# Gate and up projections ahead of the query projection in a decode kernel

## The chip, the cores and the metric

The kernel runs on one core of one Trainium2 chip. The metric is the device time of one execution in microseconds (us); three runs of the kernel before gave 228.95, 229.00 and 229.19, median 229.0. A profile is of one execution. MB are millions of bytes.

## What is computed

Two parallel branches of one decode step share a layer norm: attention over the last 4096 cached positions, with 32 query heads on 8 key/value heads, and a gated MLP. All data are float32, batch B = 2, one token, D = 512, head size 128, F = 1792.

```python
xn = _layernorm(x, axis=-1)
# attention
q = (xn @ wq).reshape(B, Sq, 32, 128)
k = k_cache[:, :, Sk - 4096:, :]        # each kv head serves 4 query heads
v = v_cache[:, :, Sk - 4096:, :]
p = softmax(einsum(q, k) * 128 ** -0.5)
attn = (p @ v).reshape(B, Sq, 4096) @ wo
# gated MLP
gate, up = xn @ W_gate, xn @ W_up
h = gate * (gate > 0) * up
return x + attn + h @ W_down
```

## The kernel before

**The stream.** Nearly all bytes are weights and cache tiles that are read once: wq in two halves of 4096 KB, w_gate and w_up of 3584 KB each, eight k tiles and eight v tiles of 4096 KB, w_down, and wo. They all go through one pool of four buffers, `ring` (L53, RING = 4), in program order, and SP issues their DMAs in that order (`load`, L69 to 72). The fifth load takes the first buffer, and so on in turn: a load waits on SP until the work that reads the buffer's old tile is done, and all later loads wait behind it. Only x comes on ACT's queue (L106).

**The opening.** DVE, ACT and PE do the layer norm; eight small matmuls (L193) transpose xn into xnT in two layouts. Then PE multiplies xnT with wq, 16 matmuls per half (L205), into two PSUM tiles. In the profile each float32 matmul shows as two records, so a half is "x32". For each tile r, ACT or DVE copies it to SBUF (qs, L213), four PE transposes turn it (qt, L216), and 16 small copies, in turn on ACT and DVE, place it into qz (L227), the zero-padded weights of the score matmuls. Then come gate and up: 16 matmuls each (L235), a copy on ACT (L240), and on DVE the gating (L242, L244) and a transpose into hT (L245). hT is not read until the projection with w_down near the end (L431).

**The attention loop.** There are four groups g (kv heads 0 to 3 or 4 to 7, of one batch row), each with two k tiles and two v tiles. `keys(g, a, ...)` transposes a k tile on DVE in two pieces (kT, L259), and after each piece PE does eight score matmuls with qz (L264; "x16" in the profile). When both k tiles of a group are through, `softmax(g)` goes from DVE over PE and ACT (L276 to 296) and `turn(g)` turns the probabilities on DVE (L302, L308). `values(g, a, v)` does the matmuls with a v tile one group later (L327). Each engine works in program order. Group 0's two k tiles come first, then for g = 1, 2, 3 and a = 0, 1 a k tile of group g and a v tile of group g - 1, then the last two v tiles, w_down and wo.

**Which slot is whose.** In the kernel before, wq's two halves, w_gate and w_up are loads 1 to 4; k0 a=0, k0 a=1, k1 a=0 and v0 a=0 are loads 5 to 8 and take their buffers. Load 9 (k1 a=1) takes the buffer of k0 a=0 when DVE has transposed it, load 10 (v0 a=1) that of k0 a=1, load 11 (k2 a=0) that of k1 a=0, load 12 (v1 a=0) that of v0 a=0 when PE has used it. Names such as k2_0 below mean group 2, a = 0.

**The end.** The projections with w_down and wo accumulate in PSUM (L431, L435); wo's last rows come in small pieces (L450, L456); DVE copies the result (L469) and SP writes it out (L471).

Of the kernel before, what the change touches and what calls it, by code (L numbers as in the profile page):

```python
# [9 lines left out]
F32 = mybir.dt.float32  # L10
AF = mybir.ActivationFunctionType
ALU = mybir.AluOpType
# [8 lines left out]
def kernel(  # L21
# [12 lines left out]
    nc = tc.nc  # L34
    P = 128
# [6 lines left out]
    KC = D // P  # L42
# [3 lines left out]
    Q = 4  # L46
# [8 lines left out]
    FB = F // P  # L55
    FQ = F // Q
# [5 lines left out]
    work = ctx.enter_context(tc.tile_pool(name="work", bufs=2))  # L62
    ps_kt = ctx.enter_context(tc.tile_pool(name="ps_kt", bufs=3, space=PSUM))
# [5 lines left out]
    def load(name, src, shape):  # L69
        t = ring.tile(shape, F32, name=name, tag="ring")  # L70
        nc.sync.dma_start(t, src)
        return t


    def load_wq(m):
        src = wq[m * 2 * P:(m + 1) * 2 * P, :].rearrange("(p k) f -> p k f", p=P)
        return load(f"wq{m}", src, [P, 2, HQ * DH])

    def load_ff(w, name):
        return load(name, w.rearrange("(p k) f -> p k f", p=P), [P, KC, F])  # L80
# [23 lines left out]
    x2 = const.tile([B, D], F32, name="x2")  # L104
    for half in (slice(0, D // 2), slice(D // 2, D)):
        nc.scalar.dma_start(x2[:, half], x[:, 0, half])  # L106
    wqt = [load_wq(m) for m in range(2)]

    ident = const.tile([P, P], F32, name="ident")
# [13 lines left out]
    hT = const.tile([P, FB, 32], F32, name="hT")  # L123
# [34 lines left out]
    for h in range(2):  # L158
        nc.vector.tensor_reduce(
            out=by_h[:, :, h], in_=ident[:, PK * h:PK * h + PK].rearrange("p (x t k) -> p t k x", t=NP, k=REP),  # L160
            op=ALU.add, axis=AX.X,
# [25 lines left out]
    for kc in range(KC):  # L187
        m, k = divmod(kc, 2)
# [7 lines left out]
    xnT = const.tile([P, 2, KC, 32], F32, name="xnT")  # L196
    nc.vector.tensor_copy(xnT, xt_ps)


    q_ps = [ps_kt.tile([P, 512], F32, name=f"q_ps{r}", tag="kt") for r in range(R)]  # L200
    for kc in range(KC):
        for r in range(R):
            for c in range(C):
# [2 lines left out]
                    q_ps[r][32 * c:32 * c + 32, :], xnT[:, 0, kc, :], wqt[kc // 2][:, kc % 2, n * 512:(n + 1) * 512],  # L206
                    start=(kc == 0), stop=(kc == KC - 1),
                )
    gw = load_ff(w_gate, "wg")
    uw = load_ff(w_up, "wu")  # L210
    for r in range(R):
        qs = work.tile([P, 512], F32, name=f"qs{r}", tag="qs")
        (nc.vector.tensor_copy if r else nc.scalar.copy)(qs, q_ps[r])  # L213
# [5 lines left out]
        for m in range(NB):  # L219
            src = qt[32 * m:32 * m + 32, :, :, 0].rearrange("p i (t h) b -> p b t h i", h=2)  # L220
            for x in range(Q):
                d = qz[32 * x:32 * x + 32, r * B:r * B + B, m]
                dst = bass.AP(
                    tensor=d.tensor, offset=d.offset + x * TK,
                    ap=[d.ap[0], d.ap[1], [64 + REP, NP], [32, 2], [1, REP]],
                )
                (nc.vector.tensor_copy if x % 2 else nc.scalar.copy)(dst, src)  # L227


    g_ps = ps_kt.tile([P, FQ], F32, name="g_ps", tag="kt")  # L230
    u_ps = ps_kt.tile([P, FQ], F32, name="u_ps", tag="kt")
    for dst, wt in ((g_ps, gw), (u_ps, uw)):
        for kc in range(KC):
            for c in range(Q):
                nc.tensor.matmul(  # L235
                    dst[32 * c:32 * c + 32, :], xnT[:, 1, kc, :], wt[:, kc, c * FQ:(c + 1) * FQ],
                    start=(kc == 0), stop=(kc == KC - 1),
                )
    gs = work.tile([P, FQ], F32, name="gs", tag="qs")
    nc.scalar.copy(gs, g_ps)  # L240
    gr = gs
    nc.vector.scalar_tensor_tensor(gr, gs, 0.0, gs, op0=ALU.is_gt, op1=ALU.mult)  # L242
    hh = work.tile([P, FQ], F32, name="hh", tag="qs")
    nc.vector.tensor_tensor(hh, gr, u_ps, op=ALU.mult)  # L244
    nc.vector.transpose(hT, hh.rearrange("p (w k) -> p k w", k=FB))  # L245

    ss, pts = {}, {}
# [197 lines left out]
    for r, cuts in ((0, (0, NJ)), (1, (0, 4, 8, 12, 14, 15))):  # L447
        wt = ring.tile([P, NJ, D], F32, name=f"wo{r}", tag="ring")
# [53 lines left out]
```

## Time and profile before

| what | value |
|---|---|
| median of three runs | 229.0 us |
| the profiled execution's own time | 228.95 us |
| its span in the trace | 227.2 us |
| PE busy | 129.8 us (57%) |
| DVE busy | 118.7 us (52%) |
| ACT busy | 14.3 us (6%) |
| bytes read from HBM | 94.90 MB |

Times in the trace count from the start of the span. PE, DVE, ACT and POOL are the engines for matmuls, vector work, activations and the rest; PEld is PE's loading of weights; "SPq" rows are DMAs that SP issues, with the time at which it does. In a timeline row stand the start, the length, the engine, the line, out<-in, the shapes and the count; in square brackets the engine's idle time before it and what ended it. In a row of windows stand the bounds, the length, the busy time of PE, PEld, DVE, ACT and POOL with the number of their instructions, then PE's granted clock (1.00 is full), the DMA engines' mean share (packets are counted where they begin, so a short window can go over 1) and the GB/s.

### The profile page before, as it was taken

What the parts mean: (1) busy time and instruction counts of PE and PEld (TensorE: products, weight loads), DVE (VectorE), ACT (ScalarE), POOL (GpSimd) and SP (SyncE); (2) the same over time, 40 slices, a digit from 0 to 9 for tenths busy, and PEclk for the clock granted to TensorE, in tenths of its full rate; (3) what the DMA queues carried; (4) which work ended last, traced back from release to release, by engine and by line L of the source; (5) the groups of instructions that cost most, each with busy time, mean ns of one, the idle gap of its engine ahead of it and who ended that gap; (6) DMA issues with size and microseconds to landing.
All of it is one profiled execution on the core that took longest, in us unless ns stands there. A gap on an engine that the chain in (4) does not pass through costs nothing.

```text
span 227.2 us, 2137 instructions
## 1 busy us (share of the span) xinstructions
PE 129.8 (57%) x896; PEld 39.2 (17%) x896; DVE 118.7 (52%) x160; ACT 14.3 (6%) x41; POOL 4.2 (2%) x14
## 2 busy tenths in 40 slices
PE   0195754803656003886815984607937644988694
PEld 0161220200101001221201321101501201221313
DVE  2400142039892399973599894699269286013000
ACT  2000231000000500000200000200000110000001
POOL 7000000000000000000000000000000000000000
PEclk9999979675876655896675899955996996599769
DMA  7999999999999999999999999999999999999992
GB/s 277 462 398 421 454 434 413 462 421 415 456 440 398 450 462 404 424 462 404 424 462 415 421 456 433 407 450 450 415 427 456 410 424 462 408 428 453 385 415 74
DMA packets 4212, 95.03 MB, mean 418 GB/s; under 512 B 488, under 2 KB 748, under 8 KB 1004
## 3 DMA queue, kind: packets, MB, share of 16 engines
q1 hardware_dynamic: 4196, 94.90, 97.3%
q8 instruction: 7, 0.11, 0.2%
q14 instruction: 1, 0.01, 0.0%
q10 hardware_dynamic: 8, 0.00, 0.0%
HBM read 94.90 MB, written 0.00 MB: 418 GB/s over the span
## 4 chain that ended last, share of the span: by engine, by line
DMA 50%; DVE 26%; PE 17%; issue 3%; ACT 2%; SPq 0%; DVEq 0%; ACTq 0%
DMA k<-in_A_k_cache_dram 28%; DVE kT L259 17%; DMA wo<-in_A_wo_dram 13%; DMA wq<-in_A_wq_dram 9%; PE s L264 7%; DVE pt L308 4%; PE yw_ps L431 3%; PE o L327 3%; PE q_ps L205 2%; ACT pz L296 1%; DVE pT L302 1%; PE y_ps L435 1%; DVE m L276 1%; DVE on L336 1%; PE oa L347 1%
## 5 line engine op out<-in xcount | busy, mean ns | idle before, releaser
L264 PE MATMUL s<-kT,qz 128*32 128x512 f32 x256 | 44.5, 822 | 55.8 <-DVE kT L259 55.7
L259 DVE STREAM_TRANSPOSE kT<-k 128x4096 f32<-128x4096 f32 x16 | 70.5, 4428 | 10.7 <-DMA k<-in_A_k_cache_dram 10.6
L327 PE MATMUL o<-v,pt 128*32 128x512 f32 x256 | 34.5, 672 | 0.0
L264 PEld LDWEIGHTS s<-kT,qz 128*32 128x32 f32 x256 | 8.8, 130 | 84.9 <-issue 60.1
L308 DVE COPY pt<-pT 32x256 f32<-32x256 f32 x64 | 18.2, 284 | 1.0
L347 PE MATMUL oa<-on,pick 128*16 128x512 f32 x16 | 10.1, 721 | 6.9 <-DVE on L336 6.9
L327 PEld LDWEIGHTS o<-v,pt 128*32 128x32 f32 x256 | 9.6, 121 | 19.4 <-issue 19.4
L336 DVE TENSOR_TENSOR on<-o,own_u 128x512 f32<-128x512 f32 x8 | 5.4, 676 | 12.7 <-PE o L327 12.6
L227 DVE COPY qz<-qt 32x32 f32<-32x32 f32 x16 | 3.0, 187 | 16.7 <-ACT qz L227 16.7
L296 ACT ACTIVATE pz<-s,nm 64x512 f32<-64x512 f32 x8 | 5.9, 732 | 80.0 <-DVE nm L290 79.8
L205 PE MATMUL q_ps<-wq,xnT 128*32 128x512 f32 x64 | 8.8, 698 | 3.0 <-DMA wq<-in_A_wq_dram 2.5
L193 PE MATMUL xt_ps<-rep,xc 2*128 2x32 f32 x16 | 3.7, 402 | 10.7 <-DVE rep L186 10.7
L302 DVE STREAM_TRANSPOSE pT<-pz 128x1024 f32<-128x1024 f32 x4 | 5.0, 1245 | 8.3 <-ACT pz L296 8.3
L431 PE MATMUL yw_ps<-wo,oT 128*2 128x512 f32 x48 | 7.9, 831 | 1.9 <-DMA wo<-in_A_wo_dram 1.9
L276 DVE TENSOR_REDUCE m<-s 128x1 f32<-128x512 f32 x4 | 2.8, 692 | 11.6 <-PE s L264 11.6
L469 DVE COPY yo<-y_ps 128x128 f32<-128x128 f32 x1 | 0.3, 290 | 16.4 <-PE y_ps L435 16.4
L235 PE MATMUL u_ps<-wu,xnT 128*32 128x448 f32 x32 | 4.9, 781 | 4.3 <-DMA wu<-in_B_W_up_dram 4.3
L193 PEld LDWEIGHTS xt_ps<-rep,xc 2*128 2x128 f32 x16 | 3.6, 319 | 10.7 <-DVE rep L186 10.7
L235 PE MATMUL g_ps<-wg,xnT 128*32 128x448 f32 x32 | 4.9, 769 | 0.0
L244 DVE TENSOR_TENSOR hh<-gs,u_ps 128x448 f32<-128x448 f32 x1 | 0.6, 620 | 7.9 <-PE u_ps L235 7.9
L347 PEld LDWEIGHTS oa<-on,pick 128*16 128x16 f32 x16 | 1.6, 112 | 15.2 <-DVE on L336 9.8
L365 PEld LDWEIGHTS op<-osb,spread 16*128 16x128 f32 x32 | 3.7, 186 | 1.8 <-issue 1.8
(72 smaller groups left out, 56.4 us busy)
## 6 DMA issues: line engine op xcount, KB each, us to landing
k<-in_A_k_cache_dram SPq DMA_DIRECT2D x8, 4096.0 KB, 24.4
v<-in_A_v_cache_dram SPq DMA_DIRECT2D x8, 4096.0 KB, 28.9
wq<-in_A_wq_dram SPq DMA_DIRECT2D x2, 4096.0 KB, 16.7
wo<-in_A_wo_dram SPq DMA_DIRECT2D x1, 4096.0 KB
wg<-in_B_W_gate_dram SPq DMA_DIRECT2D x1, 3584.0 KB, 29.3
wu<-in_B_W_up_dram SPq DMA_DIRECT2D x1, 3584.0 KB, 38.6
wd<-in_B_W_down_dram SPq DMA_DIRECT2D x1, 3584.0 KB, 28.0
wo<-in_A_wo_dram SPq DMA_DIRECT2D x3, 1024.0 KB, 18.8
```

Source lines behind the costliest of these rows:

```text
L193: nc.tensor.matmul(xt_ps[:, v, kc, :], lhsT, rep16.rearrange("r s b -> r (s b)"), start=True, stop=True)
L205: nc.tensor.matmul(q_ps[r][32 * c:32 * c + 32, :], xnT[:, 0, kc, :], wqt[kc // 2][:, kc % 2, n * 512:(n + 1) * 512], start=(kc == 0), stop ...
L235: nc.tensor.matmul(dst[32 * c:32 * c + 32, :], xnT[:, 1, kc, :], wt[:, kc, c * FQ:(c + 1) * FQ], start=(kc == 0), stop=(kc == KC - 1),)
L259: nc.vector.transpose(kt.rearrange("p j m i -> p j (m i)"), src)
L264: nc.tensor.matmul(ss[g][32 * q:32 * q + 32, :], qz[:, g, 2 * mh + m, a, h], kt[:, JS * s1:JS * s1 + JS, m, h::2], start=(a == 0 and mh == ...
L296: nc.scalar.activation(pv[o, :, :, h], ss[g][o].rearrange("p (j i) -> p j i", j=JS), AF.Exp, bias=nm[o], scale=SCALE, accum_out=l[o],)
L302: nc.vector.transpose(pT.rearrange("p j x t k -> p (j x t k)"), pz.rearrange("p j s -> p (j s)"))
L308: nc.vector.tensor_copy(pts[g][32 * x:32 * x + 32, :, s1, :, h], pT[q:q + 32, :, x].rearrange("p j t k -> p t j k"))
L327: nc.tensor.matmul(o[32 * q:32 * q + 32, :], pts[g][:, a, s1, j:j + 4].rearrange("p u h k -> p (u h k)"), v[:, lo:lo + 512], start=(s1 == ...
L336: nc.vector.tensor_tensor(ons[a], o.rearrange("p (u d) -> p u d", u=4), own_u[:, :, None].to_broadcast([P, 4, P]), op=ALU.mult)
L347: nc.tensor.matmul(oa[g].rearrange("h u d -> h (u d)"), pick[:, 8 - 8 * a:24 - 8 * a], ons[a].rearrange("p u d -> p (u d)"), start=(a == 0 ...
L431: nc.tensor.matmul(yw_ps[32 * c:32 * c + B, :], lhsT, w, start=(n < Q), stop=(n >= wide - Q))
```

## The change

The loads of w_gate and w_up go ahead of those of wq, and the matmuls and the elementwise steps of gate and up go ahead of the query projection. Nothing is added or left out; the lines of the steps move, by one or two elsewhere.

```diff
     for half in (slice(0, D // 2), slice(D // 2, D)):
         nc.scalar.dma_start(x2[:, half], x[:, 0, half])
+    gw = load_ff(w_gate, "wg")
+    uw = load_ff(w_up, "wu")
     wqt = [load_wq(m) for m in range(2)]
...
     nc.vector.tensor_copy(xnT, xt_ps)
+    g_ps = ps_kt.tile([P, FQ], F32, name="g_ps", tag="kt")
+    u_ps = ps_kt.tile([P, FQ], F32, name="u_ps", tag="kt")
+    for dst, wt in ((g_ps, gw), (u_ps, uw)):
+        for kc in range(KC):
+            for c in range(Q):
+                nc.tensor.matmul(
+                    dst[32 * c:32 * c + 32, :], xnT[:, 1, kc, :], wt[:, kc, c * FQ:(c + 1) * FQ],
+                    start=(kc == 0), stop=(kc == KC - 1),
+                )
+    gs = work.tile([P, FQ], F32, name="gs", tag="qs")
+    nc.scalar.copy(gs, g_ps)
+    gr = gs
+    nc.vector.scalar_tensor_tensor(gr, gs, 0.0, gs, op0=ALU.is_gt, op1=ALU.mult)
+    hh = work.tile([P, FQ], F32, name="hh", tag="qs")
+    nc.vector.tensor_tensor(hh, gr, u_ps, op=ALU.mult)
+    nc.vector.transpose(hT, hh.rearrange("p (w k) -> p k w", k=FB))
     q_ps = [ps_kt.tile([P, 512], F32, name=f"q_ps{r}", tag="kt") for r in range(R)]
...
-    gw = load_ff(w_gate, "wg")
-    uw = load_ff(w_up, "wu")
     for r in range(R):
         qs = work.tile([P, 512], F32, name=f"qs{r}", tag="qs")
...
-    g_ps = ps_kt.tile([P, FQ], F32, name="g_ps", tag="kt")
...
-    nc.vector.transpose(hT, hh.rearrange("p (w k) -> p k w", k=FB))
```

The start of SP's queue, as a difference; wq_81 to wq_87 are the two halves of wq, wg and wu the gate and up weights, and k_0_272 and k_1_295 the two k tiles of group 0:

```order
-L71 DMA wq_81<-in_A_wq_dram 128x8192
-L71 DMA wq_83<-in_A_wq_dram 128x8192
 L71 DMA wg<-in_B_W_gate_dram 128x7168
 L71 DMA wu<-in_B_W_up_dram 128x7168
+L71 DMA wq_85<-in_A_wq_dram 128x8192
+L71 DMA wq_87<-in_A_wq_dram 128x8192
 L71 DMA k_0_272<-in_A_k_cache_dram 128x1x8192
 L71 DMA k_1_295<-in_A_k_cache_dram 128x1x8192
```

The halves of wq have moved from the first two places to the third and fourth, so the ring's first two buffers now hold w_gate and w_up; all later loads stand as before.

DVE from the copy of xnT to the first two k transposes, before; qt and q_ps are the PSUM tiles of the query, kT_0_0 and kT_0_1 the pieces of group 0's first k tile:

```order
L197 COPY xnT<-xt_ps 128x256
L227 COPY qz<-qt_188 32x2x2x2x4 x8
L213 COPY qs_209<-q_ps_149 128x512
L227 COPY qz<-qt_211 32x2x2x2x4 x8
L242 SCALAR_TENSOR_TENSOR gs<-gs 128x448
L244 TENSOR_TENSOR hh<-gs,u_ps 128x448
L245 STREAM_TRANSPOSE hT<-hh 128x448
L259 STREAM_TRANSPOSE kT_0_0_275<-k_0_272 128x4096
L259 STREAM_TRANSPOSE kT_0_1_285<-k_0_272 128x4096
```

And the same place on DVE in the changed kernel:

```order
L199 COPY xnT<-xt_ps 128x256
L214 SCALAR_TENSOR_TENSOR gs<-gs 128x448
L216 TENSOR_TENSOR hh<-gs,u_ps 128x448
L217 STREAM_TRANSPOSE hT<-hh 128x448
L245 COPY qz<-qt_228 32x2x2x2x4 x8
L231 COPY qs_249<-q_ps_193 128x512
L245 COPY qz<-qt_251 32x2x2x2x4 x8
L258 STREAM_TRANSPOSE kT_0_0_275<-k_0_272 128x4096
L258 STREAM_TRANSPOSE kT_0_1_285<-k_0_272 128x4096
```

The 16 qz copies and the qs copy now stand between hT and the k transposes, where they had stood ahead of the three steps of gate and up.

More of the change, by code (lines that the diff above doesn't have):

```diff
@@ L227 @@
                 (nc.vector.tensor_copy if x % 2 else nc.scalar.copy)(dst, src)
-    g_ps = ps_kt.tile([P, FQ], F32, name="g_ps", tag="kt")
[L231 to L244, printed above, removed]
-    nc.vector.transpose(hT, hh.rearrange("p (w k) -> p k w", k=FB))
     ss, pts = {}, {}
```

## The prediction

> **What bounds the kernel now.** I read the page first: utilisation in 40 slices, DMA queues, chain.
>
> ```profile
> span 227.2 us, 2137 instructions
> DMA  7999999999999999999999999999999999999992
> GB/s 277 462 398 421 454 434 413 462 421 415 456 440 398 450 462 404 424 462 404 424 462 415 421 456 433 407 450 450 415 427 456 410 424 462 408 428 453 385 415 74
> q1 hardware_dynamic: 4196, 94.90, 97.3%
> DMA 50%; DVE 26%; PE 17%; issue 3%; ACT 2%; SPq 0%; DVEq 0%; ACTq 0%
> ```
>
> The DMA digits are 9 from the second slice to the last but one. The chain names DVE for 26%, but that only says who released a ring slot; the transfer it released queued behind others. Next, windows: long ones for the rate, and ones that begin at zero to count what had been moved when a load was first used.
>
> ```profile
> 0.00:22.55 22.55, 8.85 (x48) 4.72 (x48) 4.16 (x17) 1.58 (x2) 4.20 (x14) 1.00 0.94 393
> 0.00:60.20 60.20, 27.85 (x176) 10.00 (x180) 18.80 (x39) 5.53 (x20) 4.20 (x14) 0.86 0.98 418
> 0.00:92.91 92.91, 39.83 (x235) 12.17 (x235) 43.52 (x65) 8.38 (x25) 4.20 (x14) 0.78 0.99 423
> 22.00:92.00 70.00, 30.64 (x187) 7.45 (x187) 38.45 (x47) 6.80 (x23) 0.00 (x0) 0.72 1.00 432
> 92.00:202.00 110.00, 70.80 (x471) 20.09 (x468) 74.14 (x92) 5.05 (x13) 0.00 (x0) 0.81 1.00 433
> ```
>
> The last column is GB/s: 432 and 433 over two long stretches, DMA share 1.00. The rate does not depend on what PE or DVE do. The end hangs on the same stream: the last weight load for y_ps waits 0.16 us for a piece of wo, and the output leaves right behind it.
>
> ```profile
> 223.90 0.13 PEld L435 LDWEIGHTS y_ps<-wo,oT_rows 128*17 128x17 f32 x8 [0.16 <-DMA wo<-in_A_wo_dram]
> 224.60 0.69 SPq L471 DMA_DIRECT2D out_dram<-yo  x1
> ```
>
> So the time is the start of the stream, 94.90 MB at its rate, and a fixed tail. The change moves no byte count. It can matter only if the queue runs dry, and for that I read the SP timeline (issue times) and the sizes.
>
> ```profile
> wq<-in_A_wq_dram SPq DMA_DIRECT2D x2, 4096.0 KB, 16.7
> wg<-in_B_W_gate_dram SPq DMA_DIRECT2D x1, 3584.0 KB, 29.3
> 0.73 0.85 SPq L71 DMA_DIRECT2D wq<-in_A_wq_dram  x2
> 20.11 17.04 SPq L71 DMA_DIRECT2D k<-in_A_k_cache_dram  x3
> 45.80 0.54 SPq L71 DMA_DIRECT2D v<-in_A_v_cache_dram  x1
> 59.27 0.53 SPq L71 DMA_DIRECT2D k<-in_A_k_cache_dram  x1
> 69.03 0.53 SPq L71 DMA_DIRECT2D v<-in_A_v_cache_dram  x1
> 92.91 0.53 SPq L71 DMA_DIRECT2D k<-in_A_k_cache_dram  x1
> 98.56 0.54 SPq L71 DMA_DIRECT2D v<-in_A_v_cache_dram  x1
> ```
>
> In MB of a million bytes, wq halves, k and v tiles are 4.19 each, w_gate and w_up 3.67 each. Before the issue at 92.91 (k2_0, first half of group 2) the queue had been given 15.73 for the four weights and 6 x 4.19 for k and v, 40.89 in all. By 92.91 it had begun 423 x 92.91 = 39.30. What remains, 1.59 MB, lasts 3.7 us at 432. Done the same way, the next issue (98.56) has 45.09 MB queued against about 41.7 begun, 7.8 us; at 59.27 it is 32.50 against 418 x 59.27 = 24.8, 18 us. **The issue of k2_0 is the one thin place, with 3.7 us.** It waits for a slot that DVE frees.
>
> **The change, part by part.**
>
> *The four weight loads in another order.* Same four transfers, same sum of 15.73 MB, all issued without a wait near 0.7 to 2.7 us. Whatever lands fourth lands when w_up did. Cost: 0 to the stream.
>
> *The gate/up matmuls first.* They take over the time that the first q half had, under the loading of wq. Their ACT and DVE steps are then done while DVE would stand still; nobody waits for hT before the end of the kernel. The three slots freed by PE in this stage come within a few us of their old times, against 18 us and more of queued bytes: cost 0.
>
> *The q chain last.* Here lies the cost. These are the rows, PE and DVE timeline:
>
> ```profile
> 22.55 3.64 PE L205 MATMUL q_ps<-wq,xnT 128*32 128x512 f32 x32 [2.51 <-DMA wq<-in_A_wq_dram]
> 35.02 0.20 DVE L227 COPY qz<-qt 32x32 f32<-32x32 f32 x1 [0.24 <-ACT qz L227]
> 40.83 4.91 PE L235 MATMUL u_ps<-wu,xnT 128*32 128x448 f32 x32 [4.28 <-DMA wu<-in_B_W_up_dram]
> 50.47 8.77 DVE L259 STREAM_TRANSPOSE kT<-k 128x4096 f32<-128x4096 f32 x2 [3.07 <-DMA k<-in_A_k_cache_dram]
> 60.23 8.77 DVE L259 STREAM_TRANSPOSE kT<-k 128x4096 f32<-128x4096 f32 x2 [0.99 <-DMA k<-in_A_k_cache_dram]
> 59.39 2.05 PE L264 MATMUL s<-kT,qz 128*32 128x512 f32 x16 [0.69 <-DVE kT L259]
> 69.06 3.64 PE L264 MATMUL s<-kT,qz 128*32 128x512 f32 x16 [1.49 <-DVE kT L259]
> 84.11 13.10 DVE L259 STREAM_TRANSPOSE kT<-k 128x4096 f32<-128x4096 f32 x3
> 40.00:42.00 2.00, 1.17 (x12) 0.42 (x16) 0.00 (x0) 0.00 (x0) 0.00 (x0) 0.97 1.10 475
> 42.00:44.00 2.00, 2.00 (x16) 0.65 (x12) 0.00 (x0) 0.00 (x0) 0.00 (x0) 0.50 1.18 508
> 70.00:72.00 2.00, 2.00 (x16) 0.30 (x8) 0.00 (x0) 0.00 (x0) 0.00 (x0) 0.50 1.21 524
> ```
>
> 1. wq's second half now lands at 40.8, where w_up did. Its 32 records are 512 wide. The nearest row is u_ps: 4.91 x 512/448 = 5.6 us, so q ends at 46.4. The bounds are the full-clock row, 3.64 us (44.5), and twice that (48.1): the granted clock (third column from the end) is 0.97 and then 0.50 inside the u_ps burst.
> 2. From the end of q to the last qz copy it took 35.22 - 26.19 = 9.0 us, a ping-pong of ACT and DVE with two rounds of transposes. It was hidden under weight loading. Now it ends at 55.4, and DVE, which runs in order, cannot begin the k transposes at 50.47 as before. Queued behind it on DVE are all kT transposes, and PE and SP wait for those.
> 3. The first two transposes (8.77) end at 64.2 instead of 59.24; the second tile, there since 60.2, follows at once and ends at 73.0 instead of 69.0. One gap of 0.99 us has swallowed part. DVE is now 4.0 us late.
> 4. The last score batch before the softmax took 3.64 us at clock 0.50; at full clock such a batch takes 2.05. Shifted by 4 us against the clock, it may be either: lateness 4.0 or 2.4. I take the middle, 3.2, as the batches in the trace come in both lengths.
> 5. The softmax chain and the next two transposes are unchanged, so k2_0 goes out at 92.91 + 3.2 = 96.1.
>
> The Trainium skill, "TensorE: Matmul & The Clock Gate" (Part 1), says that the gate judges activity in free-running windows of about 3.4 us and that an idle one halves the clock. By that rule q's second half, after more than 4 us of idleness, would run one window at half speed and the rest at full, 3.4 + 1.9 = 5.3 us instead of my 5.6; the row above, with its drop at 42 and not at 40.83, agrees with free-running windows.
>
> **Is 96.1 late?** When an empty queue is given work, packets do not start at once: issue at 0.73, first packets at 1.75 to 2.25 (rows of a quarter microsecond; the last one is of the second packets).
>
> ```profile
> 1.75:2.00 0.25, 0.00 (x0) 0.00 (x0) 0.00 (x0) 0.25 (x1) 0.25 (x1) 1.00 4.39 1180
> 2.00:2.25 0.25, 0.00 (x0) 0.00 (x0) 0.00 (x0) 0.25 (x1) 0.25 (x1) 1.00 1.89 524
> 3.75:4.00 0.25, 0.00 (x0) 0.00 (x0) 0.00 (x0) 0.00 (x0) 0.25 (x2) 1.00 2.73 1180
> ```
>
> That is 1.2 us. An average DMA engine runs out at 92.91 + 3.7 = 96.6, so an issue by 95.4 costs it nothing: margin 2.5 us. The Trainium skill, "DMA: Bandwidth & Descriptors" (Latency and other measured facts), gives about 0.6 us to the first byte; by it the margin would be 3.1. No run here shows 0.6.
>
> But the engines are not in step. At 22.55, when both wq halves (8.39 MB) had landed, 8.86 had been begun, 0.47 more. At 60.20, when six loads (24.12 MB) had landed, it was 25.16, 1.04 more. One partition's row of a tile is 4096/128 = 32 KB; one such packet on each of 16 engines is 0.52 MB, 1.2 us at 432. So from then on the slowest engine is about one packet behind the mean. Its own row would be dry only 1.2 us later: margin 3.7. A load is complete when its slowest engine is, and so is the kernel. With 3.2 us of lateness the faster engines pause for 0.7 us, the slowest does not pause, and the end stays.
>
> *Afterwards.* DVE stays about 3 us late up to the long wait below, 6.58 us for a k tile, which takes it all; from there the stream sets the pace again.
>
> ```profile
> 166.84 4.45 DVE L259 STREAM_TRANSPOSE kT<-k 128x4096 f32<-128x4096 f32 x1 [6.58 <-DMA k<-in_A_k_cache_dram]
> ```
>
> **Sum:** stream 0 + weights 0 + q chain 0 (3.2 of lateness against 3.7 of margin), so the profiled 228.95 us (span 227.2 and 1.75 around it) stays. It is the lowest of three runs; the median is 229.0, and that is the forecast. Its own range is 228.6 to 229.4, which is the 0.2% that a measurement of this kernel can tell from no change.
>
> **The rivals.**
>
> *A bubble in the stream at 97 us (slower).* If the mean engine counts, because lagging engines catch up while others pause or because the lag lies elsewhere, every us of lateness over 2.5 is lost to the end: nothing later makes up for lost DMA time at share 1.00. Lateness 3.2 gives 0.7, so 229.7. Lateness 4.0 gives 1.5, and the refill may add 0.7, since the second packets at the start came 1.9 us behind the first (3.75 to 4.00) instead of 1.2: 230.5 to 231.2. It decides from a lateness of about 3.0 on. For it: the only thin place of the trace. Against it: the lag counted above, and a last score batch that may get shorter.
>
> *q wholly at half clock (slower still).* 7.3 us for q's second half make the lateness up to 5.7; even the slowest engine loses 2.0: 231. Against it: the full-clock stretch at the head of the u_ps burst.
>
> *An earlier start (faster).* The x rows share the queues with the first weight, whose rows shrink from 32 KB to 3584/128 = 28, so x and xnT may come some tenths earlier, and the first slots come free earlier. At share 1.00 that has no taker; at the most a tighter start gives 0.6 us: 228.4.
>
> **How the numbers follow.** No change that can be told: 0.55. Bubble: 0.33. Half clock: 0.05. Faster: 0.07. So faster 0.07, same 0.55, slower 0.38. The range goes from 228.5 to 230.8; it leaves out the half-clock case, the worst fifth of the bubble case and half of the faster one, about 0.15.
>
> **What would show it.** In the profile after: last qz copy near 55.4 and the first kT right behind it; second kT pair ending near 73; the k issue that stood at 92.91 near 96; windows near 97 that keep their GB/s, or show a hole in the bubble case; DVE's wait for k of 6.58 shrunk by the lateness; last piece of wo at the same 223.9. I am wrong if k2_0 goes out before 94 or after 97.5, if a hole shows and the end moves by as much, or if the end moves without one.

## The result: slower by 0.75%

The changed kernel took 230.68 us (median of six runs, 230.28 to 231.73), the kernel before 229.03 (six runs, 228.92 to 229.19). The ratio is 1.0075, with a 95% interval from 1.006 to 1.009. The forecast had been no change, 229.0; the time lies in the stated range and in the rival's, a bubble in the stream at 97 us (229.7 to 231.2).

### The profile after

First the page of the changed kernel. The profiled execution took 231.73 us, the slowest of the six, so it shows the loss at its largest.

```profile
span 229.8 us, 2136 instructions
DMA  7999999999999999899999999999999999999990
GB/s 260 449 414 434 450 442 439 399 451 445 439 399 446 445 439 405 368 411 399 456 445 428 402 456 439 433 402 456 439 416 422 456 436 397 448 444 431 384 385 27
q1 hardware_dynamic: 4196, 94.90, 96.6%
```

There is one 8 among the nines, in slice 17, from 91.9 to 97.7 us; its 368 GB/s is the lowest figure between the first slice and the last; the ends of the kernel apart, no other is below 397. Next SP's issues in the same trace, around the one that matters.

```profile
47.24 0.54 SPq L71 DMA_DIRECT2D v<-in_A_v_cache_dram  x1
65.49 0.54 SPq L71 DMA_DIRECT2D k<-in_A_k_cache_dram  x1
74.14 0.54 SPq L71 DMA_DIRECT2D v<-in_A_v_cache_dram  x1
96.42 0.54 SPq L71 DMA_DIRECT2D k<-in_A_k_cache_dram  x1
102.46 0.54 SPq L71 DMA_DIRECT2D v<-in_A_v_cache_dram  x1
```

k2_0 goes out at 96.42 instead of 92.91, 3.5 us late. What the stream did there is read from windows. The first two rows are of the kernel before, up to 90 us and from 90 to 110 us:

```profile
0.00:90.00 90.00, 37.49 (x227) 11.95 (x231) 40.61 (x64) 8.38 (x25) 4.20 (x14) 0.79 0.99 424
90.00:110.00 20.00, 15.32 (x105) 4.36 (x101) 13.59 (x8) 0.46 (x1) 0.00 (x0) 0.84 0.98 422
```

And the same two stretches of the changed kernel:

```profile
0.00:90.00 90.00, 37.80 (x219) 12.21 (x219) 36.98 (x63) 8.37 (x25) 4.21 (x14) 0.76 0.99 424
90.00:110.00 20.00, 14.76 (x94) 3.66 (x98) 15.76 (x5) 0.00 (x0) 0.00 (x0) 0.76 0.96 399
```

Up to 90 us both kernels have moved the same, at 424 GB/s. Then the changed one moves 23 GB/s less over 20 us, 0.46 MB or 1.1 us of stream. That is the hole. Now the steps that lead to it, on PE and DVE of the changed kernel.

```profile
30.17 6.54 PE L225 MATMUL q_ps<-wq,xnT 128*32 128x512 f32 x32 [6.50 <-DMA wq<-in_A_wq_dram]
40.85 6.32 PE L225 MATMUL q_ps<-wq,xnT 128*32 128x512 f32 x32 [4.14 <-DMA wq<-in_A_wq_dram]
74.17 2.06 PE L263 MATMUL s<-kT,qz 128*32 128x512 f32 x16 [2.27 <-DVE kT L258]
56.47 0.20 DVE L245 COPY qz<-qt 32x32 f32<-32x32 f32 x1 [0.24 <-ACT qz L245]
56.69 17.42 DVE L258 STREAM_TRANSPOSE kT<-k 128x4096 f32<-128x4096 f32 x4
87.62 13.10 DVE L258 STREAM_TRANSPOSE kT<-k 128x4096 f32<-128x4096 f32 x3
169.43 4.45 DVE L258 STREAM_TRANSPOSE kT<-k 128x4096 f32<-128x4096 f32 x1 [2.73 <-DMA k<-in_A_k_cache_dram]
```

The last qz copy ends at 56.67, the first k transpose follows at once, and all four of group 0 run without a gap, to 74.11. The last score batch is a short one, 2.06 us. The transposes that free k2_0's slot begin at 87.62, where they had begun at 84.11. Much later DVE waits 2.73 us for a k tile, where it had waited 6.58. Last, the end of the trace.

```profile
226.59 0.13 PEld L434 LDWEIGHTS y_ps<-wo,oT_rows 128*17 128x17 f32 x8 [0.18 <-DMA wo<-in_A_wo_dram]
227.28 0.68 SPq L470 DMA_DIRECT2D out_dram<-yo  x1
```

The last piece of wo is waited for until 226.59 instead of 223.90: 2.7 us, as much as this execution is longer (2.78). So the end still hangs on the stream, and lost more than the hole of 1.1.

### The profile page after: what moved, and what is told of

It is laid out like the page before. It is cut to its first block, busy times and chain, and to the rows that moved or that the text cites. A ratio compares the mean times of both kernels' runs of the same rounds, so it can differ in the third digit from the quotient of the medians.

```text
span 229.8 us, 2136 instructions
## 1 busy us (share of the span) xinstructions
PE 132.2 (58%) x896; PEld 39.0 (17%) x896; DVE 118.8 (52%) x160; ACT 14.3 (6%) x41; POOL 4.2 (2%) x14
## 4 chain that ended last, share of the span: by engine, by line
DMA 38%; DVE 31%; PE 19%; issue 4%; ACT 4%; SPq 1%; DVEq 0%; ACTq 0%
DVE kT L258 19%; DMA wq<-in_A_wq_dram 17%; DMA k<-in_A_k_cache_dram 12%; DMA wo<-in_A_wo_dram 10%; PE s L263 7%; DVE pt L307 6%; PE o L326 5%; PE q_ps L225 3%; ACT pz L295 2%; DVE pT L301 2%; PE oa L346 2%; DVE qz L245 1%; ACT qz L245 1%; DVE on L335 1%; DVE m L275 1%
## 5 line engine op out<-in xcount | busy, mean ns | idle before, releaser
L326 PE MATMUL o<-v,pt 128*32 128x512 f32 x256 | 33.0, 648 | 0.0
L225 PE MATMUL q_ps<-wq,xnT 128*32 128x512 f32 x64 | 12.9, 978 | 10.6 <-DMA wq<-in_A_wq_dram 10.6
L346 PE MATMUL oa<-on,pick 128*16 128x512 f32 x16 | 10.8, 766 | 6.9 <-DVE on L335 6.9
L326 PEld LDWEIGHTS o<-v,pt 128*32 128x32 f32 x256 | 8.8, 117 | 18.9 <-issue 18.8
L430 PE MATMUL yw_ps<-wo,oT 128*2 128x512 f32 x48 | 7.0, 748 | 2.1 <-DMA wo<-in_A_wo_dram 2.1
L225 PEld LDWEIGHTS q_ps<-wq,xnT 128*32 128x32 f32 x64 | 2.8, 168 | 20.5 <-DMA wq<-in_A_wq_dram 12.7
L207 PE MATMUL g_ps<-wg,xnT 128*32 128x448 f32 x32 | 5.4, 850 | 0.5 <-DVE xnT L199 0.5
L234 PE MATMUL qt<-ident,qs 128*128 128x128 f32 x8 | 1.7, 356 | 4.4 <-DVE qs L231 4.4
L364 PE MATMUL op<-osb,spread 16*128 16x32 f32 x32 | 3.9, 273 | 0.0
## 6 DMA issues: line engine op xcount, KB each, us to landing
wg<-in_B_W_gate_dram SPq DMA_DIRECT2D x1, 3584.0 KB, 11.2
```

The costliest lines, as they stand in the source:

```text
L225: nc.tensor.matmul(q_ps[r][32 * c:32 * c + 32, :], xnT[:, 0, kc, :], wqt[kc // 2][:, kc % 2, n * 512:(n + 1) * 512], start=(kc == 0), stop ...
L326: nc.tensor.matmul(o[32 * q:32 * q + 32, :], pts[g][:, a, s1, j:j + 4].rearrange("p u h k -> p (u h k)"), v[:, lo:lo + 512], start=(s1 == ...
L346: nc.tensor.matmul(oa[g].rearrange("h u d -> h (u d)"), pick[:, 8 - 8 * a:24 - 8 * a], ons[a].rearrange("p u d -> p (u d)"), start=(a == 0 ...
L364: nc.tensor.matmul(op, spread.rearrange("h k e -> h (k e)")[:, NE - 1 - e:NE - 1 - e + P], osb[r][:, :, e * NJ:(e + 1) * NJ].rearrange("h ...
```

## The experiments

**Theory A** says that the stream runs dry near 97 us because k2_0 is issued late, and that each engine's own pause counts. A second form of it, with which I had forecast, has the margin of the slowest engine, 3.7 us. **Theory B** says that the new order of loads or matmuls costs something as such. All comparisons are with runs of the kernel before on the same chip.

### The lateness taken out of the changed kernel: q1act

The second tile's part of the query chain goes to ACT alone; all else is the changed kernel.

```diff
-        (nc.vector.tensor_copy if r else nc.scalar.copy)(qs, q_ps[r])
+        nc.scalar.copy(qs, q_ps[r])
...
-                (nc.vector.tensor_copy if x % 2 else nc.scalar.copy)(dst, src)
+                (nc.vector.tensor_copy if x % 2 and r == 0 else nc.scalar.copy)(dst, src)
```

> The changed kernel, with the second half of the query chain (the qs1 copy and its 16 small qz copies) given to ACT alone, so that DVE is free for the first k transpose after the first eight qz copies, near 51.3 us instead of 56.7. The lateness of the k2_0 issue (96.42 in the changed kernel, 92.91 before) should fall from 3.5 to about 0 to 1 us. Theory A (the stream runs dry at 97 us because k2_0 is issued late): no hole at 97, 229.0 to 229.4 us, ratio to the kernel before within 0.998 to 1.002. Theory B (the cost comes from the new order of the loads or of the matmuls as such, and k2_0 only happens to be late): 230.3 to 230.9 us, as the changed kernel.

It took 229.03 us against 229.13, ratio 0.9998 (0.999 to 1.0007). The rows are DVE's first k transposes, SP's issue of k2_0 and the window at the hole:

```profile
51.25 8.77 DVE L258 STREAM_TRANSPOSE kT<-k 128x4096 f32<-128x4096 f32 x2
92.50 0.54 SPq L71 DMA_DIRECT2D k<-in_A_k_cache_dram  x1
90.00:110.00 20.00, 15.43 (x105) 3.91 (x101) 13.19 (x8) 0.41 (x1) 0.00 (x0) 0.82 0.99 426
```

DVE is free 5.4 us earlier, k2_0 is on time, the hole is gone, and with it the whole loss, though w_gate and w_up are still loaded and used first. Theory B falls for the change as made.

The control, the same edit in the kernel before (before_q1act):

> Control for q1act: the kernel before with the same edit (second half of the query chain on ACT alone). There the chain is hidden under the loading of the weights, so k2_0 stays near 92.9. Theory A: 229.0 to 229.2 us, ratio 0.998 to 1.002. If the edit itself saved time, this would come out at 228.5 or less, and the cure in q1act would not speak for the late issue alone.

229.03 against 228.99, ratio 1.0002 (0.9993 to 1.0011). The edit gains nothing of its own.

### The lateness put into the kernel before: the late series

Before the transposes that free k2_0's slot, DVE repeats the hT transpose n times, 0.97 us each; loads and opening stay as before.

```diff
     softmax(0)
     turn(0)
+    for _ in range(n):
+        nc.vector.transpose(hT, hh.rearrange("p (w k) -> p k w", k=FB))
```

> The kernel before with one idle 0.94 us repeat of the hT transpose ahead of the k transposes that free the slot of k2_0; issue near 93.9 at the latest. Theory A (the stream runs dry, every engine for itself; late2 lost in some executions and not in others): inside the margin, 229.0 to 229.2 us and a narrow spread. Theory A with a margin of 3.7: the same.

> The kernel before, with two idle repeats of the 0.94 us hT transpose on DVE between the first softmax and the k transposes that free the slot of k2_0: k2_0 goes out about 1.9 us later, near 94.9. Both theories: under the margin of the mean engine (2.5 us), so 229.0 us, ratio 0.998 to 1.002. A loss here would say that the margin was reckoned too wide.

> Three repeats, 2.9 us. Between late2 (229.25) and late4 (230.93). Theory A with every engine's own pause counting: 229.8 to 230.6 us. With the slowest engine's margin of 3.7 us: 229.0 to 229.2.

> As late2 with four repeats: k2_0 about 3.9 us late, near 96.8, a little later than in the changed kernel, with the loads and the opening as before. Theory A, margin 2.5 us for every engine and a refill of up to 0.7: 230.4 to 231.1 us, with a hole of about 1.4 us in the stream at 97. Theory A with a margin of 3.7, the slowest engine's: 229.2 us. Theory B: 229.0 to 229.2 us.

> As late2 with six repeats: k2_0 about 5.8 us late, near 98.7. Theory A, margin 2.5 for every engine: 3.3 us of hole and up to 0.7 of refill, 232.3 to 233.0 us. With the slowest engine's margin of 3.7: 231.1 us. Theory B: the kernel before has no other cost here, 229.0 to 229.3 us.

> Ten repeats, 9.7 us, or 8.1 where the last score batch comes out short as it did in late4 and late6. late6 went out at 97.0, 4.1 us late, and lost 2.2 us, so lateness less 2.0 goes to the end. Theory A: 6.1 to 7.7 us lost, 235.1 to 236.8 us, a hole of 6 us or more, and a tail after the hole no longer than the kernel before has, since all engines start again together. With the slowest engine's margin of 3.7: 233.4 to 235.1.

The issue time, the GB/s from 90 to 110 us and the one time are of the profiled execution.

| n | k2_0 issued (late by) | GB/s 90 to 110 | that execution, us | median, us | before, us | ratio (95%) |
|---|---|---|---|---|---|---|
| 1 | 93.62 (0.7) | 422 | 229.19 | 229.04 | 229.03 | 1.0005 (0.9996 to 1.0014) |
| 2 | 94.51 (1.6) | 415 | 231.11 | 229.25 | 229.13 | 1.0029 (1.0006 to 1.0051) |
| 3 | 94.15 (1.2) | 419 | 230.29 | 230.18 | 229.03 | 1.0054 (1.0035 to 1.0073) |
| 4 | 94.93 (2.0) | 419 | 231.18 | 230.93 | 229.13 | 1.0074 (1.0054 to 1.0094) |
| 6 | 97.01 (4.1) | 386 | 231.02 | 231.36 | 229.13 | 1.0103 (1.0081 to 1.0125) |
| 10 | 102.43 (9.5) | 271 | 236.32 | 234.98 | 229.03 | 1.0273 (1.0253 to 1.0294) |

The issue rows and windows of two of them, first late4, then late10:

```profile
94.93 0.53 SPq L71 DMA_DIRECT2D k<-in_A_k_cache_dram  x1
90.00:110.00 20.00, 15.39 (x99) 4.31 (x99) 14.97 (x6) 0.00 (x0) 0.00 (x0) 0.79 0.98 419
```

```profile
102.43 0.53 SPq L71 DMA_DIRECT2D k<-in_A_k_cache_dram  x1
90.00:110.00 20.00, 11.19 (x80) 3.21 (x81) 17.89 (x9) 0.00 (x0) 0.00 (x0) 0.65 0.65 271
```

Three things follow. Lateness alone makes the loss, in a kernel with the old order: late4 loses what the change loses. From n = 6 to n = 10 it goes to the end one for one: between the two profiled executions the issue moves by 5.4 us and the time by 5.3. And the loss begins inside the margin of 2.5 us, let alone 3.7: the profiled executions of late3 and late4, 1.2 and 2.0 us late, take 1.3 and 2.1 us more than the median of before. The lateness in the trace is up to 1.9 us less than the repeats add up to, because the last score batch before the softmax comes out short in some executions; how late the other executions were is not known.

Three runs came out otherwise than expected. late2 lost where no loss was expected. late6 lost 2.2 us where Theory A had at least 3.2; its k2_0 was 4.1 us late in the profiled execution instead of 5.8, so that its time lies near the 231.1 of the second form for another reason. The median of late10 lies 0.1 us under Theory A's range.

late2 shows what the mean hides. Its runs lie between 228.92 and 231.59, and its profiled one, 2.0 us over the median of before, has a small hole: 415 against 422 GB/s is 0.14 MB, 0.3 us. The end of its trace shows the rest, beside the end of before:

```profile
222.00:224.00 2.00, 1.59 (x32) 0.64 (x28) 0.00 (x0) 0.58 (x1) 0.00 (x0) 1.00 0.53 199
224.00:226.00 2.00, 1.94 (x67) 1.14 (x58) 0.00 (x0) 0.00 (x0) 0.00 (x0) 1.00 0.13 43
```

```profile
222.00:224.00 2.00, 2.00 (x80) 1.60 (x72) 0.00 (x0) 0.59 (x1) 0.00 (x0) 1.00 0.34 121
224.00:226.00 2.00, 0.21 (x8) 0.04 (x7) 0.29 (x1) 0.00 (x0) 0.00 (x0) 1.00 0.01 2
```

The kernel before is done with its loads by 224. late2 still moves at 13% of the DMA engines' time after that, while 87% stands idle: a few engines are about 2 us behind the others.

The control for the series has four repeats one step later (late4_next), behind the transposes that free the slot of k2_0:

```diff
             keys(g, a, kt_in, steps)
+            if g == 1 and a == 0:
+                for _ in range(4):
+                    nc.vector.transpose(hT, hh.rearrange("p (w k) -> p k w", k=FB))
```

> Control for the late series: the same four repeats (3.9 us of DVE) one step further on, behind the two k transposes that free the slot of k2_0. So k2_0 goes out at 92.9 as before, and it is the issues after it, with 7.8 us and more of queued bytes, that are late by up to 3.9 us. Theory A: 229.0 to 229.2 us, 433 GB/s or so around 97, ratio 0.998 to 1.002. If a DVE that is late as such costs the end something, this comes out like late4, 230.5 to 231 us.

228.98 against 229.09, ratio 0.9993 (0.9984 to 1.0002). Issue of k2_0, the k issue after next, and the window:

```profile
91.46 0.54 SPq L71 DMA_DIRECT2D k<-in_A_k_cache_dram  x1
104.61 0.54 SPq L71 DMA_DIRECT2D k<-in_A_k_cache_dram  x1
90.00:110.00 20.00, 13.57 (x104) 3.57 (x101) 15.82 (x12) 0.86 (x3) 0.00 (x0) 0.93 0.99 425
```

The same work on DVE costs nothing there. It is a weaker control than meant: k2_0 came 1.5 us early in this execution, so the later k issue, at 103.64 before, was only 1.0 us late.

### Half of the change: gate1

w_gate alone is loaded and used first, then wq, then w_up.

```diff
+    gw = load_ff(w_gate, "wg")
     wqt = [load_wq(m) for m in range(2)]
...
+    g_ps = ps_kt.tile([P, FQ], F32, name="g_ps", tag="kt")
...
+    nc.vector.scalar_tensor_tensor(gr, gs, 0.0, gs, op0=ALU.is_gt, op1=ALU.mult)
     q_ps = [ps_kt.tile([P, 512], F32, name=f"q_ps{r}", tag="kt") for r in range(R)]
...
-    gw = load_ff(w_gate, "wg")
     uw = load_ff(w_up, "wu")
```

> Half of the change: w_gate is loaded and used first, then wq, then w_up. The query chain is over before w_up has landed, near 45 us, so DVE can take the first k tile at 50.5 as before and k2_0 goes out near 92.9. Theory A: 229.0 to 229.2 us, ratio 0.998 to 1.002. Theory B (the order of the loads costs as such): 229.6 to 230.0, about half of the loss.

229.49 against 229.03, ratio 1.0021 (1.0012 to 1.0031): a miss for Theory A. Issue and window:

```profile
92.83 0.53 SPq L71 DMA_DIRECT2D k<-in_A_k_cache_dram  x1
90.00:110.00 20.00, 15.39 (x109) 4.47 (x105) 13.51 (x8) 0.68 (x2) 0.00 (x0) 0.84 0.99 427
```

k2_0 is on time and there is no hole, so in this execution at least the cost is another one. It is the fastest of the nine, and what the others would show is not known. The same kernel with q1act's edit was to tell whether it comes from DVE in the opening:

> The half change of gate1 with the edit of q1act. gate1 lost 0.46 us without a late k2_0 and without a hole. If that comes from DVE being held in the opening, it goes: 229.0 to 229.1 us. If it comes from the split of gate and up or from the program as such, it stays: 229.4 to 229.6 us.

229.78 against 228.99, ratio 1.0029 (1.0019 to 1.004): it stays, so it isn't DVE in the opening. Over all runs the median span is 227.5 us for gate1 and 227.9 for gate1_q1act against 227.2 for the kernel before, so most of the loss lies within the span. What it is stays open. The edit of gate1 also gives gs another buffer (tag "on" instead of "qs"), which no run tests by itself. The full change with q1act's edit does not have this cost.

## Why the forecast was wrong

**Right: the stream, and the place.** The new order of the loads costs nothing by itself (q1act); the one thin place is the issue of k2_0; nothing lost there is made up later, and DVE's lateness ends in its wait for a k tile (6.58 to 2.73).

**Near, but partly by luck: the lateness.** 3.5 us instead of 3.2, with two errors against each other. q ended at 47.17 and not 46.4, and with qz the first k transpose came at 56.69 and not 55.4; the second pair ended 5.1 us late and not 4.0. But the last score batch took 2.06 us, the short bound and not the middle.

**q's clock.** Both halves of q took 6.3 to 6.5 us, between my 5.6 and the bound of 7.3. Rows of windows of the changed kernel, the third column from the end being the granted clock:

```profile
40.00:42.00 2.00, 1.15 (x8) 0.40 (x12) 0.00 (x0) 0.00 (x0) 0.00 (x0) 0.50 1.14 492
42.00:44.00 2.00, 2.00 (x12) 0.39 (x8) 0.00 (x0) 0.00 (x0) 0.00 (x0) 0.50 1.10 475
44.00:46.00 2.00, 2.00 (x16) 0.42 (x12) 0.00 (x0) 0.00 (x0) 0.00 (x0) 0.50 0.76 328
46.00:48.00 2.00, 1.76 (x16) 0.59 (x8) 0.00 (x0) 0.74 (x2) 0.00 (x0) 0.92 1.18 508
```

The 0.92 of the last row stands for about 0.3 us at 0.50, so the burst ran at half clock from 40.85 to about 46.3, some 5.4 us. The Trainium skill, "TensorE: Matmul & The Clock Gate" (Part 1), says that the gate opens after a sustained busy window of about 3.4 us and that windows don't wait for the burst. The trace agrees: a burst that begins within a window pays for the rest of that one and then for a whole one. I had counted 3.4 us from its start.

**Wrong: the margin.** The step was: "With 3.2 us of lateness the faster engines pause for 0.7 us, the slowest does not pause, and the end stays." The late series shows executions that lose with 1.2 to 2.0 us of lateness, so there was no margin of 3.7, and even 2.5, reckoned for the mean engine, was too much. The step took the lag of the slowest DMA engine for a cushion, and it took the 1.2 us from an issue to its first packets to be the same on all engines.

The traces also keep 16 landing times for each load and the start and length of every DMA packet. Each packet of k2_0 is 32 KB and takes 1.21 us in the steady stream. In the changed kernel fourteen engines end v0_1, the load before k2_0, by 97.87, and fourteen first packets of k2_0 begin between 97.74 and 98.18, 1.3 to 1.8 us after the issue. The lag was there: the other two engines end v0_1 at 98.45 and 98.48. One of these goes on at once, at 98.49. The other, which the forecast had as safe, stands still until 100.07, 3.6 us after the issue, and its first packet takes 2.48 us. (The records don't name engines, but all other starts come before these two are done, so these two starts are theirs.) That engine lands its part of k2_0 last, and the lateness stays to the end. The last landing of three loads, in the profiled executions:

| kernel | v0_1, us | k2_0, us | last piece of wo, us |
|---|---|---|---|
| before | 99.0 | 108.7 | 223.9 |
| changed | 98.9 | 111.4 | 226.5 |
| q1act | 99.0 | 108.6 | 223.7 |
| late2 | 99.0 | 109.4 | 225.9 |
| late3 | 98.8 | 108.8 | 225.2 |
| late4 | 98.8 | 109.4 | 226.1 |

So the changed kernel's loss is all there when k2_0 lands: 2.7 us by one engine, where the stream as a whole lost 1.1. In late2 to late4 only 0.1 to 0.7 us is there by then. The rest comes in one later slip. In late2 it lies between two loads that land at 138.4 and 149.6, 11.2 us apart, where one k or v tile takes 9.7. In late3 it lies between 118.5 and 129.6, in late4 between 177.2 and 188.5. In each of the three a 16 KB fetch of instructions (queue q8, seven of them in each of these executions) begins shortly before the late landing: at 146.5, 127.6 and 185.4. The kernel before has such fetches too, but at those that follow k2_0's landing its last landing moves by no more than 0.3 us.

Two things stay open: why one engine gets its new packets so much later than the others (in late10, where all 16 stood still, all begin within 1.3 to 1.9 us of the issue), and whether it is the fetch that delays the last landing in late2 to late4, and why it does not in the kernel before. These records are of one execution for each kernel; whether the others lost their time in the same way is not known.

## What to carry to other kernels

In a kernel bound by its stream of loads, work out at each issue how many microseconds of bytes are still queued; the smallest figure says how far a change may delay the engine that frees that slot. Work hidden under the loading of one weight is not hidden under the loading of another: here 9 us of small copies moved to where an in-order engine had the next tile waiting. Leave an issue more room than the mean of the engines asks for, since the one that fares worst sets the end: in the profiled executions 3.0 us of queued bytes (3.7 less 0.7) were enough, and 2.5 (3.7 less 1.2) were not.

## What the runs showed of the hardware

- In these single executions the end reacts in a step, not in proportion: 0.7 us of lateness cost nothing that can be told, while executions with 1.2 to 2.0 us lost 1.3 to 2.1 us, and one with 4.1 us lost about as much (1.9, against 229.13).
- A queue that is nearly dry can leave one DMA engine behind the rest: in the changed kernel one begins k2_0 at 100.07 and fourteen by 98.18, and the end loses 2.7 us where the stream as a whole lost 1.1. A queue that is wholly dry costs the end as much as the stream: late10's window lacks 151 GB/s over 20 us, 3.0 MB or 7.0 us, and that execution took 7.3 us more than 229.03.
